# Weights of a soft mixture of experts loaded as whole experts: 2 MB transfers with 16 KB rows instead of 1 MB with 8 KB rows

## The chip, the cores and the metric

The kernel runs on one core of a Trainium2 chip. The metric is the device time of one execution in microseconds (us). On one core, a run is called slow when it is over 1.5% above the fastest run of its kernel. Six runs of the kernel before spread over 0.26 us (178.22 to 178.48), so small steps below were run several times in rounds that alternate with the kernel before, on the same chip.

## The reference, cut to what matters

Eight batches of eight heads of local attention (four heads with a window of 32, four with a dilated window), 576 tokens each, feed a soft mixture of experts with 8 experts of 4 slots.

```python
logits = x @ phi                                   # x: attention output, 4608 x 512
d = softmax of logits over the tokens
slot_input = (d.T @ x).reshape(E, S_per_e, D)      # needs all of the attention
for e in range(E):                                 # w1[e]: 512 x 1024, w2[e]: 1024 x 512, float32
    h = np.maximum(slot_input[e] @ w1[e], 0.0)
    slot_out[e] = h @ w2[e]
return softmax of logits over the slots @ slot_out # 4608 x 512 float32
```

Two things follow. The experts can't start until the attention has ended, and the output can't start until the last expert has its weights. q, k and v are 28.3 MB, w1 and w2 together 33.6 MB, the output 9.4 MB.

## The kernel before

The loads issued from POOL, all on one queue, are cast from float32 to bf16 on the way: the page of the kernel before has 30.41 MB written by that queue. Only phi and the first half expert come from SP (1.1 MB, not cast). The program is laid out at build time by a list scheduler: every operation has a priority, made of the number of its half batch (`PERIOD`) and an offset for its kind (`OFFS`); the scheduler runs a model of the engines and of the loads, and so fixes the order of instructions on each engine. Each engine then works through its list in order and waits where data is missing, as PE does 1.62 us before the first slab's work (timeline of the kernel before, below).

```python
W_AFTER = [0, 1, 1, 1, 1, 1, 1, 1, 1, 1, 1, 1, 1, 1, 1, 99]   # weight transfers after each half batch's k, q, v
PERIOD = 21.8
OFFS = dict(T=92.2, SC=104.1, EX=-30.5, MK=78.7, ...)

def w1_piece(e, hf, r0=0, n=2):                 # half an expert: partition p gets rows 2p and 2p+1, 8 KB
    def fn():
        return pool.dma_start(
            a(o_w1 + e * 4096 + hf * 2048 + 1024 * r0, [[1, 1024 * n]]),
            moe_w1[e, 256 * hf:256 * hf + 256, :].rearrange("(p two) f -> p (two f)", two=2)
            [:, 1024 * r0:1024 * (r0 + n)])
    ...
def w2_piece(e, c0):                            # half of an expert: 8 KB out of each 16 KB
    ...
def w2_slab(e, s, c0=0, n=8):                   # half of the output columns: rows of 1 KB
    ...
for e in range(8):
    wq += [w1_piece(e, x) for x in range(e == 0, 2)]
for e in range(6):
    wq += [w2_piece(e, 0), w2_piece(e, 4)]
for s in range(2):                              # experts 6 and 7: columns 0-255 first, then the rest
    wq += [w2_slab(6, s), w2_slab(7, s, 0, 4), w2_slab(7, s, 4, 2),
           w2_slab(7, s, 6, 1), w2_slab(7, s, 7, 1)]
```

The tail: `sd_fn` transposes the slot inputs (four small transposes on PE, the first work after the attention), `l1_fn` is the first expert layer (64 matmuls), `l2` the second. The last two experts' second weights come in two slabs of columns. When slab 0 is there, the left half of the output is computed for 2.5 of 9 token groups and stored ("early stores", rows of 1 KB); when slab 1 is there, the right half of the same groups and then whole rows of the others follow. The number of early groups is `NA = 2.5`.

The softmax here doesn't subtract the row's maximum and nothing guards it: scores larger than these inputs give would overflow.

## Time and profile before

| | before |
|---|---|
| time, median of 3 (178.22 to 178.29) | 178.27 us |
| span of the profile | 176.3 us |
| last load packet ends (from the packets in the trace file; no view prints it) | 152.2 us |
| first expert layer on PE | 128.1 to 131.8 us |
| DMA engines busy | all of the span, apart from its ends |

From the page of the kernel before: the span, the busy tenths of the DMA engines and what they wrote in 40 slices of 4.4 us, the packets, and the bytes at the memory.

```profile
span 176.3 us, 4802 instructions
...
DMA  5999999999999999999999999999999999999997
GB/s 182 237 211 213 216 207 213 214 209 213 215 208 214 214 208 214 214 207 215 210 209 213 211 211 216 213 216 210 217 213 211 210 192 194 298 319 415 416 427 316
DMA packets 19221, 41.26 MB, mean 234 GB/s; under 512 B 1921, under 2 KB 8577, under 8 KB 18305
...
HBM read 61.93 MB, written 9.44 MB: 405 GB/s over the span
```

The GB/s are of bytes written. A cast load writes half of what it reads (30.41 MB for 60.8 of the 61.93 MB read; the rest is SP's), so 212 GB/s in the slices of the loads are 424 GB/s read. The dip to 192 and 194 is the slabs with their 1 KB rows. Slices of 415 and more are stores, which write what they read: their transfers make 9.44 MB, as does the HBM line.

The chain of work that ended last, before: start in us, length in us, what. Its end is quoted.

```profile
119.16 33.35 DMA ar<-in_moe_w_dram
...
152.56 0.30 PE ps L858
...
152.88 0.44 DVE ar L882
...
153.81 8.63 DVE ar L914 x15
```

The last slab was issued at 119.16 us and landed 33 us later, behind everything queued ahead of it. The loads of q, k and v landed a median 21 us after their issue. So the queue is never near empty, and the end of the loads is set by bytes and by what a byte costs.

PE in the timeline of the kernel before: start, length, engine, line, operation, count, and in brackets how long PE sat idle before it and for what.

```profile
127.56 0.26 PE L802 MATMUL ps<-ar 32*128 32x32 bf16 x4 [0.77 <-DVE ar L744]
128.13 3.64 PE L819 MATMUL ps<-ar 128*32 128x512 bf16 x64 [0.32 <-DVE ar L808]
...
133.81 1.91 PE L858 MATMUL ps<-ar 128*32 128x512 bf16 x32 [0.54 <-DVE ar L843]
136.91 1.90 PE L858 MATMUL ps<-ar 128*32 128x512 bf16 x8 [1.18 <-DMA ar<-in_moe_w_dram]
...
144.43 1.05 PE L858 MATMUL ps<-ar 128*32 128x256 bf16 x8 [1.62 <-DMA ar<-in_moe_w_dram]
```

The first line is the end of the attention (127.6 us), the second the first expert layer, the third experts 0 to 3 of the second layer. From 136 us on PE waits for weights: there is slack between the attention and the weights. At 144.4 us the first slab's work begins.

### The profile page before, as it was taken

The page shows a single profiled execution, that of the slowest core. Times are in us where ns is not written, and L with a number is a line of the kernel's source. Part 1 is how long each engine was busy: PE and PEld are TensorE (multiplying, and loading weights), DVE is VectorE, ACT ScalarE, POOL GpSimd, SP SyncE. Part 2 cuts the span into 40 slices and gives each one's busy share as a digit, 9 for nine tenths or more (in the row PEclk, how much of TensorE's full clock was granted, in tenths as well). Part 3 has the DMA queues.
Part 4 walks back from the last instruction along what each step waited for, and adds up shares of the span by engine and source line. Part 5 has one row for each costly group of instructions (what it writes and reads, how often), then busy time and mean ns, then how long its engine had stood idle before and what let it go on. Part 6 is the DMA issues. An engine that isn't in the chain of part 4 may idle for free.

```text
span 176.3 us, 4802 instructions
## 1 busy us (share of the span) xinstructions
PE 126.7 (72%) x2102; PEld 85.4 (48%) x2102; DVE 119.6 (68%) x218; ACT 104.3 (59%) x165; POOL 51.1 (29%) x102
## 2 busy tenths in 40 slices
PE   0008787889798999989969989996685648897000
PEld 0005555667577767667647667674333224431000
DVE  6899396897989899999599899655400013499200
ACT  2404379888689889799669779793320012399000
POOL 7659822422422513423860000691000000000000
PEclk9999999999999999999999999999999996999855
DMA  5999999999999999999999999999999999999997
GB/s 182 237 211 213 216 207 213 214 209 213 215 208 214 214 208 214 214 207 215 210 209 213 211 211 216 213 216 210 217 213 211 210 192 194 298 319 415 416 427 316
DMA packets 19221, 41.26 MB, mean 234 GB/s; under 512 B 1921, under 2 KB 8577, under 8 KB 18305
## 3 DMA queue, kind: packets, MB, share of 16 engines
q0 software_dynamic: 15056, 30.41, 91.4%
q1 hardware_dynamic: 4144, 10.55, 15.6%
q8 instruction: 16, 0.26, 0.5%
q14 instruction: 5, 0.03, 0.0%
HBM read 61.93 MB, written 9.44 MB: 405 GB/s over the span
## 4 chain that ended last, share of the span: by engine, by line
DMA 47%; DVE 21%; PE 13%; POOL 4%; ACT 4%; issue 2%; POOLq 0%; DVEq 0%
DMA ar<-in_k_dram 28%; DMA ar<-in_moe_w_dram 19%; DVE ar L489 6%; DVE ar L914 6%; PE ps L510 4%; POOL ar L371 3%; ACT ar L549 3%; PE ps L604 2%; DVE ar L615 2%; PE ps L571 2%; DVE ar L445 2%; PE ps L517 2%; DVE ar L450 1%; PE ps L527 1%; DVE ar L495 1%
## 5 line engine op out<-in xcount | busy, mean ns | idle before, releaser
L549 ACT ACTIVATE ar<-ps 128x1152 bf16<-128x1152 f32 (+1 forms) x32 | 37.9, 1185 | 24.1 <-PE ps L534 13.4
L489 DVE STREAM_TRANSPOSE ar<-ar 128x576 uint32<-128x576 uint32 x40 | 48.6, 1241 | 3.0 <-DMA ar<-in_k_dram 2.8
L510 PE MATMUL ps<-ar 128*128 128x320 bf16 (+1 forms) x128 | 23.4, 308 | 15.7 <-DVE ar L489 13.8
L615 DVE TENSOR_TENSOR ar<-ps,fs 96x768 bf16<-96x768 f32 (+1 forms) x32 | 26.3, 822 | 1.2
L577 ACT ACTIVATE ar<-ps 128x768 bf16<-128x768 bf16 x32 | 24.9, 812 | 1.1 <-PE ps L571 1.0
L510 PEld LDWEIGHTS ps<-ar 128*128 128x128 bf16 x128 | 10.4, 100 | 20.8 <-POOL ar L418 13.7
L604 PE MATMUL ps<-ar 128*128 128x65 bf16 x320 | 15.5, 197 | 3.4 <-ACT ar L549 3.2
L571 PE MATMUL ps<-ar 128*128 128x128 bf16 x192 | 15.8, 228 | 2.8 <-DVE ar L615 1.9
L911 ACT ACTIVATE ar<-ps,fs 128x512 f32<-128x512 f32 (+1 forms) x23 | 11.5, 637 | 8.2 <-PE ps L902 8.2
L604 PEld LDWEIGHTS ps<-ar 128*128 128x128 bf16 x320 | 12.8, 100 | 6.5 <-ACT ar L549 3.8
L858 PE MATMUL ps<-ar 128*32 128x512 bf16 (+1 forms) x80 | 11.4, 352 | 5.9 <-DMA ar<-in_moe_w_dram 5.2
L335 POOL DMA_DIRECT2D ar<-in_k_dram x16 | 8.9, 554 | 23.1 <-DVE ar L489 19.7
L571 PEld LDWEIGHTS ps<-ar 128*128 128x128 bf16 x192 | 12.4, 118 | 4.3 <-DVE ar L615 2.5
L914 DVE TENSOR_SCALAR ar<-ps,fs 128x512 f32<-128x512 f32 (+1 forms) x23 | 12.7, 626 | 1.2 <-PE ps L902 1.2
L611 DVE RECIPROCAL fs<-ps 96x12 f32<-96x12 f32 (+1 forms) x32 | 6.4, 199 | 9.9 <-PE ps L604 9.3
L364 POOL DMA_DIRECT2D ar<-in_moe_w_dram x12 | 6.4, 580 | 20.8 <-DVE ar L489 20.8
L335 POOL DMA_DIRECT2D ar<-in_q_dram x16 | 8.7, 546 | 11.9 <-DVE fs L611 7.0
L902 PE MATMUL ps<-ar 128*128 128x512 bf16 (+1 forms) x46 | 10.4, 356 | 1.3 <-DVE ar L882 1.0
L335 POOL DMA_DIRECT2D ar<-in_v_dram x16 | 8.8, 549 | 8.9 <-DVE fs L611 5.5
L858 PEld LDWEIGHTS ps<-ar 128*32 128x32 bf16 x80 | 5.1, 99 | 12.0 <-DMA ar<-in_moe_w_dram 9.0
L671 ACT ACTIVATE ar<-ps 128x576 bf16<-128x576 bf16 x16 | 9.9, 656 | 1.4 <-PE ps L655 1.2
L694 PE MATMUL ps<-ar 128*128 128x288 bf16 x64 | 9.2, 287 | 1.2 <-ACT ar L678 1.2
(75 smaller groups left out, 190.6 us busy)
## 6 DMA issues: line engine op xcount, KB each, us to landing
ar<-in_moe_w_dram POOLq DMA_DIRECT2D x29, 512.0 KB, 27.0
out_dram<-ar SPq DMA_DIRECT2D x6, 1024.0 KB, 8.5
ar<-in_k_dram POOLq DMA_DIRECT2D x16, 288.0 KB, 21.1
ar<-in_q_dram POOLq DMA_DIRECT2D x16, 288.0 KB, 21.3
ar<-in_v_dram POOLq DMA_DIRECT2D x16, 288.0 KB, 21.6
out_dram<-ar SPq DMA_DIRECT2D x10, 256.0 KB, 3.5
ar<-in_moe_w_dram SPq DMA_DIRECT2D x1, 1024.0 KB, 4.8
ar<-in_moe_w_dram POOLq DMA_DIRECT2D x2, 256.0 KB, 33.0
```

Of the source, the lines that this page charges most:

```text
L335: return pool.dma_start(a(o_stg + (s * 3 + j) * 1152, [[1, 1152]]), src[b, 4 * dl:4 * dl + 4].rearrange("h (p t) d -> (h p) (t d)", p=32))
L489: return dve.transpose(au(o_dst, [[1, 18], [18, 32]]), au(src, [[32, 18], [1, 32]]))
L510: pe.matmul(pf(h, 0, [[1, W]]), a(o_id, [[1, 128]]), a(msk, [[1, W]]), start=True, stop=False)
L549: eo = op(ACT, lambda P=P, W=W: act.activation(a(P, [[W, 4], [1, W]]), AP(ps, 0, [[4096, 128], [512, 4], [1, W]]), ACTF.Exp, scale=SCALE), ...
L571: last = pe.transpose(pb(bank.idx, bb * 256 + par * 32, [[64, 4], [1, 32]]), src, a(o_id, [[1, 128]]))
L577: op(ACT, lambda t=t, bank=bank: act.activation(a(o_vb[vs] + 3 * t * VBK, [[66, 12], [2, 32], [1, 2]]), pb(bank.idx, 0, [[64, 12], [1, 32] ...
L604: last = pe.matmul(pf(bank.idx + x, 65 * t, [[1, 65]]), w, a(VB + t * VBK + 66 * h, [[1, 65]]), start=True, stop=True)
L615: op(DVE, lambda hp=hp, bank=bank: dve.tensor_tensor(a(ox + 128 * hp, [[64, 2], [256, NT], [1, 64]], 0, rows), pf(bank.idx, 0, [[512, 2], ...
L858: last = pe.matmul(pf(sobank[x].idx, 0, [[1, n]], 32 * j, 32), a(o_htz + 1024 * g + 128 * c + 32 * j, [[1, 32]]), a(w2off(e) + DM * c + co ...
L902: op(PE, lambda: pe.matmul(pf(bank.idx, 0, [[1, cw]]), a(o_et + 512 * G + j, [[4, 128]]), a(o_so + c0, [[1, cw]]), start=True, stop=True), ...
L911: op(ACT, lambda: act.activation(dst, src(), ACTF.Copy, scale=sca), actt(cw, .1), prio + .1, reads=[bank, b_rinv], writes=wr, name=f"OE{G} ...
L914: op(DVE, lambda: dve.tensor_scalar(dst, src(), sca, None, op0=AluOp.mult), dvet(cw, True) + .08, prio + .1, reads=[bank, b_rinv], writes= ...
```

## The change

Its intent: fewer and larger transfers, with longer rows. Seven pairs of w1 transfers and five pairs of w2 transfers are merged; w1's features are dealt to the partitions in fours instead of twice in twos, so that one partition's share is 16 KB in a row of memory. Seven transfers instead of fourteen go between the loads of q, k and v, and so `W_AFTER` changes; `PERIOD` and `OFFS` are set anew.

```diff
-W_AFTER = [0, 1, 1, 1, 1, 1, 1, 1, 1, 1, 1, 1, 1, 1, 1, 99]
-PERIOD = 21.8
+W_AFTER = [0, 1, 1, 0, 1, 0, 1, 0, 1, 0, 1, 0, 1, 0, 0, 99]
+PERIOD = 22.6
-OFFS = dict(T=92.2, SC=104.1, EX=-30.5, MK=78.7, ...)
+OFFS = dict(T=64.4, SC=177.5, EX=-17.6, MK=58.6, ...)
@@
+    def w1_rows(e):
+        return moe_w1[e].rearrange("(p four) f -> p (four f)", four=4)
+
+    def w1_piece(e, r0=0):
+        def fn():
+            return pool.dma_start(a(o_w1 + e * 4096 + 1024 * r0, [[1, 4096 - 1024 * r0]]),
+                                  w1_rows(e)[:, 1024 * r0:])
@@
-    for e in range(8):
-        wq += [w1_piece(e, x) for x in range(e == 0, 2)]
-    for e in range(6):
-        wq += [w2_piece(e, 0), w2_piece(e, 4)]
+    wq += [w1_piece(e, 2 if e == 0 else 0) for e in range(8)]
+    wq += [w2_piece(e) for e in range(5)] + [w2_piece(5, 0, 4), w2_piece(5, 4, 4)]
@@ the transposes of the slot inputs
-                                a(o_sdb + 256 * (c // 2) + c % 2, [[2, 128]], 0, 32),
+                                a(o_sdb + c, [[4, 128]], 0, 32),
```

More of the change, by code (lines that the diff above doesn't have):

```diff
@@ L26 @@
 LRU = 130.0
-OFFS = dict(T=92.2, SC=104.1, EX=-30.5, MK=78.7, TB=-29.0, VE=-46.3, PV=-36.7, RC=-26.4,
-            NM=-241.3, XT=-17.7, XE=8.2, LG=-77.2, EXL=95.9, ET=37.3, EE=30.2, SI=61.8, SA=58.7)
+OFFS = dict(T=64.4, SC=177.5, EX=-17.6, MK=58.6, TB=-42.6, VE=-89.4, PV=-21.2, RC=-6.8,
+            NM=-229.1, XT=-20.7, XE=15.1, LG=-37.0, EXL=132.1, ET=25.9, EE=0.6, SI=26.7, SA=50.4)
 class Buf:
@@ L351, in w_sem, with w2_piece @@
         return shared[key]
-    def w1_piece(e, hf, r0=0, n=2):
+    def w1_rows(e):
[4 more added lines that the diff above has]
+                                  w1_rows(e)[:, 1024 * r0:])
+        return (fn, (4 - r0) << 19, f"w1_{e}", [b_w1[e]])
+    def w2_piece(e, c0=0, n=8):
         def fn():
             return pool.dma_start(
-                a(o_w1 + e * 4096 + hf * 2048 + 1024 * r0, [[1, 1024 * n]]),
-                moe_w1[e, 256 * hf:256 * hf + 256, :].rearrange("(p two) f -> p (two f)", two=2)
-                [:, 1024 * r0:1024 * (r0 + n)])
-        return (fn, n << 19, f"w1_{e}{hf}", [b_w1[e]])
-    def w2_piece(e, c0):
-        def fn():
-            return pool.dma_start(
-                a(w2off(e) + c0 * DM, [[1, 4 * DM]]),
-                moe_w2[e].rearrange("(p c) f -> p (c f)", c=8)[:, c0 * DM:(c0 + 4) * DM])
-        return (fn, 1 << 20, f"w2_{e}{c0}", b_w2[e] if e < 5 else [b_w5h[c0 // 4]])
+                a(w2off(e) + c0 * DM, [[1, n * DM]]),
+                moe_w2[e].rearrange("(p c) f -> p (c f)", c=8)[:, c0 * DM:(c0 + n) * DM])
+        return (fn, n << 18, f"w2_{e}{c0}", b_w2[e] if e < 5 else [b_w5h[c0 // 4]])
     def w2_slab(e, s, c0=0, n=8):
@@ L400, in bass_dilated_sliding_attn__then__soft_moe_slots_kernel @@
         af(w2off(4), [[1, 2048]]),
-        moe_w1[0, 0:256, :].rearrange("(p two) f -> p (two f)", two=2)), .1, -200.0,
+        w1_rows(0)[:, :2048]), .1, -200.0,
        kind="dma", nbytes=1 << 20, sem=sem("s_w1f"), writes=b_w2[4], name="w1f")
```

## The prediction

> **What bounds the kernel now.** The loads. The slices of the page show the 16 DMA engines busy from first to last; its HBM line has 61.93 MB read and 9.44 MB written, 405 GB/s over the 176.3 us span. The windows view gives 204 to 221 GB/s written in every 3 us from 8 to 143 us, so about 424 GB/s read (the loads cast to half the bytes). The last load lands at about 152.5 us; 24 us of output follow. TensorE is busy up to 94%, but does not end last: the chain of waits runs from the loads of k to the issue of the last weight slabs, 33.4 us of DMA, then the output.
>
> **What the change does.** It merges seven pairs of w1 transfers and five of w2: 12 fewer DMAs, and 1536 pairs of 8 KB reads become 1536 reads of 16 KB. Bytes are the same. The slabs of experts 6 and 7 (1 KB rows), the halves of expert 5, the q, k, v loads and the stores stay. The new w1 order costs a stride in four small transposes. New offsets reorder PE, ACT and DVE before the tail. 1 MB less of weights lies ahead of the last q, k, v.
>
> **Cost.** Packet durations in the trace are linear in the bytes read: 60 ns for 1 KB, 192 for 4.5 KB, 324 for 8 KB: 22 ns plus 0.0368 ns per byte. Packets overlap: the busy shares sum to 1.06 with 8 KB rows and about 1.41 with 1 KB rows. So (estimates) an 8 KB row occupies an engine 324/1.06 = 306 ns where its bytes need 302, a 1 KB row 42.6 where they need 37.7: 4 to 5 ns per row is overhead. Merging saves 1536/16 = 96 rows per engine, 0.4 to 0.5 us. Each DMA ends with a 4 byte packet per engine of 22 ns: 12 fewer save at most 0.26 us. On POOL 12 issues of 0.54 us go, off the path: q, k, v land 21 us after issue, so the queue is never near empty. [...] here 1 MB transfers, queued back to back, already run at about 424, [...]. The 16 KB pitch is already that of w2, whose 8 KB rows take the same 324 ns as w1's, so I expect no penalty from it.
>
> **On the critical path.** All of the DMA saving, since loads run without a gap: the last load should land 0.4 to 0.7 us earlier, with the tail unchanged. The new engine order should be worth nothing: the second expert layer waits for weights from 135.7 us on (waits view, timeline), and has some 5 us of slack before the slabs.
>
> **Prediction: 177.6 us, range 176.9 to 178.5. Faster by over 2%: 0.02; within 2%: 0.95; slower by over 2%: 0.03.**
>
> **What would show it.** Right: 16 KB rows of about 625 ns; DMA share nearer 1.04 where they flow; last load 0.4 to 0.7 us earlier; 24 us from there to the end. Wrong: 16 KB packets over 650 ns or split in two; a stretch under 200 GB/s before the slabs; the first expert layer still running when the slabs land; a longer tail.
>
> **What would make it wrong.** A larger cost of 16 KB rows; lumpier q, k, v arrival that puts attention so far behind that staging frees late and the queue empties, or that the tail waits for it; a different start.

## The result, and the profile after

The changed kernel takes 177.91 us (177.79 to 178.15, 6 runs), the kernel before beside it 178.28 us (178.22 to 178.48, 6 runs). The ratio is 0.9978, with a 95% interval of 0.9965 to 0.9991: 0.39 us faster, small but clear of the noise. Ratios here are the mean time of one kernel's fast runs over that of the other's of the same rounds, so not quite the ratio of the medians.

From the page of the kernel after:

```profile
span 176.1 us, 4787 instructions
...
DMA  5999999999999999999999999999999999999997
GB/s 186 233 210 210 224 201 210 227 201 209 220 210 208 219 214 208 214 217 205 216 215 204 209 216 221 220 212 216 216 220 203 204 195 196 296 312 415 422 419 318
DMA packets 17492, 41.26 MB, mean 234 GB/s; under 512 B 1728, under 2 KB 8384, under 8 KB 15040
...
HBM read 61.93 MB, written 9.44 MB: 405 GB/s over the span
```

There are 1729 packets fewer: 1536 rows, 192 completion packets of 4 bytes (1665 of 4 bytes before, 1473 after, in the trace files: 16 for each of 12 transfers), and one other. The bytes are the same. Sizes count bytes written; packets of 8 KB or more grew from 916 (19221 less 18305) to 2452, by the 1536 merged rows. The slices move by a few GB/s up and down (201 to 227 from the third to the 25th, against 207 to 216), most likely because a slice of 4.4 us no longer holds whole transfers alike; no run isolates it.

The end of the chain, after:

```profile
120.13 32.05 DMA ar<-in_moe_w_dram
152.23 0.30 PE ps L857
152.55 0.44 DVE ar L881
...
153.48 8.64 DVE ar L913 x15
```

The chain ends through the same steps, and they start 0.33 us sooner. The loads end sooner by the same: the last load packet ends at 151.86 instead of 152.20 us. But PE before that looks different:

```profile
129.68 0.31 PE L801 MATMUL ps<-ar 32*128 32x32 bf16 x4 [0.77 <-DVE ar L743]
130.40 6.30 PE L818 MATMUL ps<-ar 128*32 128x512 bf16 x64 [0.41 <-DVE ar L807]
...
138.74 4.49 PE L857 MATMUL ps<-ar 128*32 128x512 bf16 x48 [0.54 <-DVE ar L842]
144.09 1.05 PE L857 MATMUL ps<-ar 128*32 128x256 bf16 x8 [0.85 <-DMA ar<-in_moe_w_dram]
```

The attention ends 2.1 us later than before, and the first expert layer takes 6.30 us instead of 3.64, because the granted clock was 0.78 and 0.71 of full speed in the 10 us stretches from 120 and 130 us, against 1.00 before; over the layer's own 6.30 us it was 0.57, and 0.50 in each microsecond of it up to 135 us. Experts 0 to 5 of the second layer no longer wait for weights: 48 matmuls run in one piece. Yet at 144.1 us PE waits for the first slab again. Five microseconds of lateness were swallowed by slack. The slower clock is not a property of the change: `x_slack` and `x_na35` (below), with the same loads, and `x_split2i` run the first expert layer in 3.64 us, and `x_bna35`, with the loads and nearly the order of before, takes 6.46 us.

The durations of single packets, which the trace records, grouped by the bytes read. They are medians over both traces and, for 2 KB, over an experiment below:

| row, bytes read | 1 KB | 2 KB | 4.5 KB | 8 KB | 16 KB | completion, 4 B |
|---|---|---|---|---|---|---|
| packet, ns | 60 | 98 | 192 | 324 | 625 | 22 |

All lie on one line of 22 ns and 0.0368 ns per byte; the 16 KB rows are where the prediction put them. A packet overlaps its neighbours (the packets' times sum to 1.06 of the 16 engines' time between 120 and 130 us before, and to 1.45 from 143 us, with 1 KB rows), so the 22 ns are not what a row costs; the experiments measure that.

The place where the loads give way to the stores, in windows of 1 us. Columns: window, its length, busy us of PE, its weight loads, DVE, ACT and POOL with counts, granted clock, DMA share, GB/s. Before:

```profile
153.00:154.00 1.00, 0.64 (x6) 0.64 (x7) 0.49 (x2) 0.30 (x1) 0.00 (x0) 1.00 1.07 368
154.00:155.00 1.00, 1.00 (x8) 0.66 (x7) 1.00 (x4) 1.00 (x4) 0.00 (x0) 1.00 0.59 206
155.00:156.00 1.00, 1.00 (x7) 0.42 (x6) 1.00 (x4) 1.00 (x3) 0.00 (x0) 1.00 0.95 325
```

After:

```profile
153.00:154.00 1.00, 0.96 (x9) 0.91 (x9) 0.52 (x2) 0.63 (x2) 0.00 (x0) 1.00 0.74 258
154.00:155.00 1.00, 1.00 (x7) 0.58 (x6) 1.00 (x3) 1.00 (x4) 0.00 (x0) 1.00 0.53 188
155.00:156.00 1.00, 1.00 (x6) 0.34 (x4) 1.00 (x3) 1.00 (x3) 0.00 (x0) 1.00 1.05 345
```

Between the early stores and those of the right halves there is a gap. Taking 1.05 as a full share, it is 0.5 us long before ((1.05 - 0.59) + (1.05 - 0.95), over 1.05) and 0.8 us after ((1.05 - 0.74) + (1.05 - 0.53), over 1.05). The early stores of the changed kernel begin at 149.49 instead of 150.23 us, more than the loads gained, so it is likely that they run out sooner for that; no run isolates it.

### The profile page after: what moved, and what is told of

Same layout as the page of the kernel before. It is cut to its first block, busy times and chain, and to the rows that moved or that the text cites. A ratio compares the mean times of both kernels' runs of the same rounds, so it can differ in the third digit from the quotient of the medians.

```text
span 176.1 us, 4787 instructions
## 1 busy us (share of the span) xinstructions
PE 129.5 (74%) x2102; PEld 86.8 (49%) x2102; DVE 120.5 (68%) x218; ACT 104.4 (59%) x165; POOL 44.9 (25%) x90
## 4 chain that ended last, share of the span: by engine, by line
DMA 32%; PE 23%; DVE 21%; ACT 10%; POOL 4%; issue 2%; POOLq 0%; DVEq 0%
DMA ar<-in_moe_w_dram 18%; DMA ar<-in_v_dram 14%; PE ps L509 6%; DVE ar L488 6%; DVE ar L913 6%; ACT ar L548 5%; POOL ar L372 3%; PE ps L603 3%; PE ps L570 3%; ACT ar L670 2%; PE ps L693 2%; DVE ar L614 2%; PE ps L516 2%; PE ps L526 2%; ACT ar L576 2%
## 5 line engine op out<-in xcount | busy, mean ns | idle before, releaser
L857 PE MATMUL ps<-ar 128*32 128x512 bf16 (+1 forms) x80 | 9.6, 338 | 2.9 <-DMA ar<-in_moe_w_dram 1.4
L693 PE MATMUL ps<-ar 128*128 128x288 bf16 x64 | 10.2, 307 | 1.2 <-ACT ar L677 1.2
L901 PE MATMUL ps<-ar 128*128 128x512 bf16 (+1 forms) x46 | 9.9, 340 | 1.3 <-DVE ar L881 1.0
L673 ACT ACTIVATE ar<-ps 128x1024 bf16<-128x1024 bf16 x8 | 8.2, 1030 | 2.5 <-PE ps L660 2.3
L494 DVE STREAM_TRANSPOSE ar<-ar 128x160 uint32<-128x160 uint32 (+1 forms) x32 | 9.5, 409 | 0.1
```

The costliest lines, as they stand in the source:

```text
L693: last = pe.matmul(pf(bank.idx, 0, [[1, 288]]), a(o_phis + 128 * c, [[1, 128]]), a(o_xt[xt] + 576 * c + 288 * g, [[1, 288]]), start=(c == ...
```

## The experiments

Theories to begin with:

- **Rows.** The gain comes from 96 rows fewer per DMA engine; a row costs 4 to 5 ns beyond its bytes (the prediction's estimate from packet times and shares).
- **DMA count.** It comes from 12 transfers fewer: completion packets, issue on POOL.
- **Order.** It comes from the new offsets, which reorder PE, ACT and DVE.

A question joined them when the first results came: what do the new offsets do, if they don't earn the gain?

### The order alone, and the loads alone

`x_order` is the kernel before with the new `PERIOD` and `OFFS`:

```diff
-PERIOD = 21.8
-OFFS = dict(T=92.2, SC=104.1, ...)
+PERIOD = 22.6
+OFFS = dict(T=64.4, SC=177.5, ...)
```

> The kernel before with only the new engine order (OFFS and PERIOD of the change), loads untouched. Rows theory (the gain comes from fewer, longer rows): 178.25 us, as before within 0.15 us, because the order of PE, ACT and DVE before the tail is off the critical path. DMA-count theory: also as before. Order theory (the retuned order earned the 0.37 us): about 177.9 us.

Measured: 179.74 us (179.47 to 179.78, 5 fast runs), ratio 1.0069 (1.0057 to 1.0082). No theory expected a loss of 1.2 us.

`x_loads` is the changed kernel with the old `PERIOD` and `OFFS`, the reverse of that edit.

> The changed kernel with the old OFFS and PERIOD, so the loads of the change alone. Rows theory and DMA-count theory: 177.9 us, the whole gain of 0.37 us. Order theory: about 178.25 us.

Measured: 182.61 us median, from 179.37 to 185.03 us. Only two of six runs count as fast (179.37 and 181.58); with them the ratio is 1.0114 (1.0062 to 1.0165). With so wide a spread this is the loss of the luckiest runs, and the usual loss may be larger. No theory expected that either. The profile is of a slow run, so its times are not used to compare; `x_order`, all of whose runs are fast, shows the mechanism. PE in the timeline of `x_order`:

```profile
137.58 0.26 PE L802 MATMUL ps<-ar 32*128 32x32 bf16 x4 [0.77 <-DVE ar L744]
138.15 3.64 PE L819 MATMUL ps<-ar 128*32 128x512 bf16 x64 [0.32 <-DVE ar L808]
143.84 4.97 PE L858 MATMUL ps<-ar 128*32 128x512 bf16 x64 [0.54 <-DVE ar L843]
149.86 1.05 PE L858 MATMUL ps<-ar 128*32 128x256 bf16 x8 [1.05 <-DMA ar<-in_moe_w_dram]
```

The loads of `x_order` are those of before, and the last load packet ends at 152.22 us, as before (152.20). But the attention ends at 137.6 instead of 127.6 us. When the first slab has landed, PE is still at experts 0 to 5; the first stores start at 152.7 instead of 150.2 us, the DMA engines run out of work between loads and stores (their share is 0.30 from 152 to 153 us, against 1.07 before), and the kernel ends later.

The reason lies in the build. I compared, place by place, the lists of PE operations (237 in each) that the scheduler makes. Before and after differ in 21 places. With the offsets exchanged, the list differs from that of the kernel whose loads it has in 146 places (`x_order` against before) and 143 (`x_loads` against after). So the new offsets do not bring a new order. They bring nearly the old order back, which the new load times would otherwise have changed for a worse one. The same comparison shows what the experiments below hold fixed: `x_2kb` has the lists of PE, ACT and DVE of the kernel before in every place, and all the `x_split` kernels have those of the change.

### How much lateness is free

From the trace of before: the second layer starts 6.2 us after the attention's end, experts 0 to 5 took 3.7 us once nothing kept them (143.8 to 147.5 us in `x_order`), and the first slab's work begins at 144.4 us. So an end of the attention up to about 134.4 us should cost nothing (an estimate from these numbers). `x_slack` tests it with the changed kernel and a third set of offsets:

```diff
-PERIOD = 22.6
-OFFS = dict(T=64.4, SC=177.5, EX=-17.6, MK=58.6, ...)
+PERIOD = 22.1
+OFFS = dict(T=83.3, SC=99.2, EX=-53.3, MK=50.4, ...)
```

> The changed kernel with a third set of offsets, for which the kernel's own schedule ends attention 4 us later than the change's and 5 us earlier than x_loads. Slack theory: the second expert layer's first six experts take 3.7 us once they start and are due at 144.4 us when the first slab lands, 6.2 us after attention's end; so an end of attention up to about 134.4 us costs nothing and this one, at about 133, takes 177.9 us within 0.2. If each us of lateness costs in proportion (x_loads: 9 us cost 1.5 to 5 us): 178.6 to 180 us. Where the throttle halves the clock during the first expert layer it comes 3 us later and may pass the edge by 1 to 2 us, with spread between runs.

Measured: 177.93 us (177.82 to 177.99, 5 fast runs), ratio 0.9975 (0.9962 to 0.9988). PE:

```profile
133.13 0.30 PE L800 MATMUL ps<-ar 32*128 32x32 bf16 x4 [0.77 <-DVE ar L742]
133.84 3.64 PE L817 MATMUL ps<-ar 128*32 128x512 bf16 x64 [0.41 <-DVE ar L806]
139.52 4.49 PE L856 MATMUL ps<-ar 128*32 128x512 bf16 x48 [0.54 <-DVE ar L841]
144.16 1.05 PE L856 MATMUL ps<-ar 128*32 128x256 bf16 x8 [0.15 <-DMA ar<-in_moe_w_dram]
```

The attention ends 3.5 us later than in the changed kernel, 64 of 237 places of the PE list differ, and the time is the same. The profile of the changed kernel had the slower clock, so its second layer starts only 0.8 us before this one (138.74 and 139.52 us); against the kernel before (133.81 us) it is 5.7 us. PE's wait for the first slab has shrunk to 0.15 us in this stretch: this kernel stands at the edge. The slack theory holds for the orders tried, and the order theory falls: an order earned nothing within the slack, and cost beyond it (`x_order`, second layer from 143.84 us).

### A dose of rows

`x_2k` keeps the number and size of the transfers of before, but fetches w1 of experts 1 to 7 and w2 of experts 0 to 4 as rows of 2 KB: each transfer takes every partition's 4 strided pieces instead of one run of 8 KB.

```diff
+    def w1_comb(e, x):
+        return pool.dma_start(a(o_w1 + e * 4096 + 512 * x, [[1024, 4], [1, 512]]),
+                              moe_w1[e].rearrange("(p four) f -> p four f", four=4)[:, :, 512 * x:512 * x + 512])
+    def w2_comb(e, x):
+        return pool.dma_start(a(w2off(e) + x * DM, [[2 * DM, 4], [1, DM]]),
+                              moe_w2[e].rearrange("(p c two) f -> p two c f", c=4, two=2)[:, x])
```

> Dose of row length: number of DMAs and bytes of each as before (1 MB pieces), but each partition of w1 of experts 1 to 7 and w2 of experts 0 to 4 is fetched as 4 strided rows of 2 KB instead of one of 8 KB. That is 576 rows more per DMA engine than in the kernel before. Rows theory at 4 to 5 ns a row: 2.3 to 2.9 us slower than before, about 180.8 us, packets of 2 KB with about 98 ns. DMA-count theory: as before, 178.3 us. Order theory: 177.9 us (it has the new order).

Measured: 181.99 us (181.70 to 184.02, 6 fast runs), ratio 1.0229 (1.0188 to 1.0270). The last load packet ends at 154.73 us, 2.53 us later than before, as the rows theory said. But 3.5 us or more of time were lost, not 2.5. I had given it the new offsets, which don't go with 1 MB transfers, and its attention ends at 138.7 us. `x_2kb` is the same with the old offsets.

> The 2 KB rows once more, now with the old OFFS and PERIOD, which go with 1 MB pieces. If x_2k lost 2.5 us by its rows (last load 154.7 instead of 152.2 us) and the other 1 us only because attention ended late (last transposes of the slot inputs at 138.7 instead of 127.6 us), this one ends attention before 131 us, has its last load at 154.7 us within 0.3, and takes 180.9 us (178.35 + 2.55). If 2 KB rows cost more than their load time, it stays near 182 us.

Measured: 180.49 us (180.36 to 180.66, 4 fast runs), ratio 1.0115 (1.0102 to 1.0128), so 2.0 us slower than before. The attention ends at 128.9 us, the last load packet at 154.56 us. The packets of its page:

```profile
DMA packets 28436, 41.26 MB, mean 231 GB/s; under 512 B 1920, under 2 KB 20864, under 8 KB 27520
```

There are 9215 packets more than before, 576 per engine, and the last load comes 2.36 us later (2.53 in `x_2k`): 4.1 to 4.4 ns per row. The total is 0.5 us better than I expected; of that 0.2 us are the load time itself. The rest is most likely the choice of the trace: the profiled run of the kernel before took 178.13 us, while its runs beside `x_2kb` took 178.22 to 178.78. Over the three traces with the loads of before (last load at 152.20, 152.22 and 152.55 us), and by the mean start of the slab packets (below), a row comes to 3.6 to 4.2 ns. If a row saved between 8 and 16 KB is worth as much as one between 2 and 8 KB, 96 rows give the change 0.4 us.

### A dose of transfers

`x_split8` cuts each of the changed kernel's 12 transfers of 2 MB into 8 of 16 neighbouring partitions. The rows stay at 16 KB.

```diff
+            return pool.dma_start(a(o_w1 + e * 4096, [[1, 4096]], 16 * y, 16),
+                                  w1_rows(e)[16 * y:16 * y + 16, :])
```

(The same is done for w2.)

> Dose of the number of DMAs: the changed kernel with each of its 12 transfers of 2 MB cut by partitions into 8 of 16 partitions, rows still 16 KB: 84 DMAs more, so 84 more 4 byte completion packets on each engine. Rows theory: as the change, 177.9 us, plus at most what those packets occupy. DMA-count theory with 22 ns a completion packet: 1.8 us slower, about 179.7 us; if the whole gain of 0.37 us over 12 DMAs were the count: 2.6 us slower, about 180.5 us. POOL spends some 40 us more on issues; if q, k, v come late by that, the load rate dips below 200 GB/s before 100 us.

Measured: 184.18 us median; the three fast runs are 181.31 to 183.39 us, ratio 1.0212 (1.0172 to 1.0252). The last load packet ends at 157.32 us, 5.5 us later than in the change, far more than 84 completion packets of 22 ns. Two more kernels take this apart, with transfers of every fourth partition (`x_split4i`, 36 DMAs more) and of every eighth (`x_split8i`, 84 DMAs more, as in `x_split8`).

```diff
+            return pool.dma_start(AP(ar, y * NBF + o_w1 + e * 4096, [[4 * NBF, 32], [1, 4096]]),
+                                  w1_rows(e)[y::4, :])
```

> The changed kernel with each 2 MB transfer cut into 4 DMAs of every fourth partition (32 partitions spread over all 128), rows still 16 KB: 36 DMAs more. x_split8 put its last load 5.5 us later for 84 more DMAs of 16 neighbouring partitions, 65 ns each. Theory A, a DMA costs that by itself: last load 2.3 us later than the change, about 154.2, time about 180.2 us. Theory B, neighbouring partitions were the cost of x_split8 and a DMA costs only its completion packets of at most 22 ns per engine: last load up to 0.8 us later, time 178.0 to 178.7 us, 16 KB packets at 625 ns on average as in the change instead of 644.

Measured: 178.43 us (178.35 to 178.52, 5 fast runs), ratio 1.0000 (0.9988 to 1.0012). The last load packet ends at 152.43 us, 0.57 us later than in the change: 16 ns per DMA and engine. The 16 KB packets are at 625 ns on average. Theory B holds.

> x_split8 with every eighth partition per DMA instead of 16 neighbours; same number of DMAs, same rows. If 84 DMAs at 15 ns are all there is: last load 1.3 us later than the change, about 153.1 us, 16 KB packets back at 625 to 630 ns from 644, time about 179.2 us. If DMAs of one row per engine cost more by their number, it stays at 157 us as x_split8.

Measured: 180.21 us (179.84 to 180.28, 4 fast runs), ratio 1.0099 (1.0085 to 1.0112). The last load packet ends at 154.14 us, 2.3 us later than in the change, 27 ns per DMA. That is a microsecond more than I expected. With one row per engine and DMA (16 rows and 16 completion packets in each), a DMA seems to cost more than with two, 27 ns against 16 (last loads are good to some 0.2 us, which is 6 ns per DMA in `x_split4i` and 2 ns here); why is open. The other 3.2 us of `x_split8` (157.32 against 154.14 us) come from which partitions a transfer takes, as that is all that differs. The GB/s of the slices show it; first `x_split8`:

```profile
GB/s 182 234 210 211 218 183 211 215 169 205 220 180 198 218 197 189 216 210 187 214 211 202 211 215 213 206 219 206 208 208 209 208 192 192 283 279 412 415 422 318
```

Then `x_split8i`:

```profile
GB/s 165 243 213 211 219 201 212 221 201 208 224 200 208 218 207 206 219 204 208 217 207 205 210 221 204 211 211 213 208 208 206 203 194 190 301 285 412 426 412 323
```

The dips to 169 to 189 GB/s, in slices in which w1 flows between q, k and v, are gone. The packets show the cost too: those of 16 KB took 644 ns on average with neighbours (`x_split8`) and 626 without (`x_split8i`). All of the lengthening lies before the last packet of q, k and v: there the 16 KB packets of `x_split8` average 660 ns, and that last packet ends at 111.1 us instead of 108.1 us. After it, when the queue holds nothing but weights, most of them still in transfers of 16 neighbours, they take 625 ns, and the loads up to 140 us run at 209.8 GB/s written (from the packets in the trace file), as in `x_split8i` (209.0). So neighbours cost 3 us where their transfers alternate with those of q, k and v, and nothing that the trace shows where they follow each other; why is open.

`x_split2i` cuts into two transfers of every second partition, so that rows are as in the change and the number of DMAs as before.

> The changed kernel with each of the 12 transfers of 2 MB cut into 2 DMAs of every second partition: rows of 16 KB, but as many DMAs as in the kernel before. It splits the change's two savings. From x_split4i (36 DMAs: last load 0.57 us later) a DMA costs about 15 ns per engine, from x_2kb and x_2k a row 4.1 to 4.4 ns. So last load 0.19 us later than the change, at about 152.0, and time 178.05 to 178.1 us: half to two thirds of the change's gain stays with the rows. If the gain were all rows: 177.9. If all the number of DMAs: 178.35, as before.

Measured: 178.12 us (178.09 to 178.16, 5 fast runs), ratio 0.9986 (0.9974 to 0.9998), against 0.9978 for the change. The last load packet ends at 152.13 us, 0.27 us later than in the change, 22 ns per DMA. By these totals about two thirds of the change's gain would be its rows and one third the number of DMAs, and the doses (0.4 us for 96 rows, 0.2 us for 12 DMAs) say about the same. But the intervals of the two ratios overlap, and the loads in the traces say the opposite. I took the fast traces together by their loads; the mean start of all 4096 slab packets is steadier than the end of the last one.

| loads | traces | last load packet ends, us | mean start of the slab packets, us |
|---|---|---|---|
| of before | before, `x_order`, `x_bna35` | 152.20, 152.22, 152.55 | 145.63, 145.56, 145.69 |
| 16 KB rows, DMAs as before | `x_split2i` | 152.13 | 145.47 |
| of the change | after, `x_slack`, `x_na35` | 151.86, 151.87, 151.75 | 145.16, 145.10, 145.16 |

The loads of the change come 0.5 us sooner in both columns. Of that, the 16 KB rows with the old number of DMAs bring 0.16 to 0.19 us and the smaller number of DMAs the other 0.3 us, from a single trace of `x_split2i`. That both rows and DMAs cost time is shown by the large doses; how the change's own gain splits between them stays open.

### The gap between early and late stores

`x_na35` is the changed kernel with 3.5 token groups stored early instead of 2.5.

```diff
-    NA = 2.5
+    NA = 3.5
-    for G, x in [(2, 2)] + [(G, x) for G in range(3, 9) for x in (0, 2)]:
+    for G, x in [(3, 2)] + [(G, x) for G in range(4, 9) for x in (0, 2)]:
```

> The changed kernel with the outputs of 3.5 groups instead of 2.5 stored in half-width pieces early. In the change the DMA share falls to 0.53 to 0.62 between 153.2 and 154.7 us (before: 0.60 to 0.73 between 154.0 and 155.5), because the early stores run out before the second half of the outputs is ready; the gap is about 0.8 us against 0.55 us, so 0.2 us of what the loads gained is lost there. If so, the longer early stores fill it, and the time is 177.3 to 177.7 us, [...]. If the gap costs nothing: 178.1 to 178.5 us.

Measured: 177.53 us (177.41 to 177.69, 5 fast runs), ratio 0.9951 (0.9938 to 0.9964). In the windows the gap is gone:

```profile
153.00:154.00 1.00, 1.00 (x10) 0.91 (x9) 0.68 (x2) 0.79 (x3) 0.00 (x0) 1.00 1.04 355
154.00:155.00 1.00, 0.94 (x6) 0.45 (x4) 1.00 (x4) 1.00 (x4) 0.00 (x0) 1.00 1.06 367
155.00:156.00 1.00, 0.96 (x5) 0.52 (x6) 1.00 (x3) 1.00 (x4) 0.00 (x0) 1.00 1.05 364
```

`x_bna35` makes the same edit in the kernel before.

> The kernel before with only the longer early stores of x_na35. Its gap between early and late stores is about 0.55 us against 0.8 us in the change, so the filling should bring less than the 0.5 us it brought there: about 178.0 to 178.2 us, and the distance between x_na35 and this one should be the load saving without the gap: 0.4 to 0.6 us. If the gap has no part in the change's small gain, this gains 0.5 us too (177.9) and the distance stays 0.37.

Measured: 178.04 us (177.79 to 178.23, 6 fast runs), ratio 0.9981 (0.9969 to 0.9993). The filling brings 0.3 us here and 0.5 us in the change (0.9978 to 0.9951). Without the gap the two load schemes lie 0.5 us apart (0.9951 over 0.9981 is 0.9970), with it 0.39 us. If so, the gap took some of what the loads gained. But each of these differences of differences is no larger than its interval. The traces make it smaller: from the end of the last load packet to the end of the span are 24.14 us before and 24.20 us in the change, and 23.87 us in both kernels with the longer early stores. So filling the gap is worth 0.3 us in either, and the wider gap of the change costs some 0.06 us.

### Fewer short rows at the end

`x_e6h` fetches half of expert 6's second weights as whole 8 KB rows before the slabs.

```diff
-    wq += ... [w2_piece(5, 0, 4), w2_piece(5, 4, 4)]
+    wq += ... [w2_piece(5, 0, 4), w2_piece(5, 4, 4), w2_piece(6, 0, 4)]
-        wq += [w2_slab(6, s), w2_slab(7, s, 0, 4), ...
+        wq += [w2_slab(6, s, 4, 4), w2_slab(7, s, 0, 4), ...
```

> The changed kernel with half of expert 6's second weights (features 0 to 3 of each 8) fetched as whole 8 KB rows in one transfer before the slabs, instead of 1 KB rows: 56 rows per engine fewer. Rows theory at 4.4 to 5 ns: last load 0.25 us earlier, at about 151.6 us. The first half of the output starts later, by 1 to 1.5 us, so that its stores reach further past the last load and fill the gap. Time 177.3 to 177.7 us if both hold; 177.9 us or more if the later start of the outputs leaves a gap of its own.

Measured: 177.89 us (177.55 to 178.40, 6 fast runs), ratio 0.9969 (0.9954 to 0.9983). The last load packet ends at 151.57 us, 0.29 us sooner than in the change, as the rows theory says. But the DMA share falls to 0.91 and 0.88 in the two windows from 149 us, against 1.35 and 1.25 in the change, with loads and early stores overlapping. The early stores come too late now, and the time is not clearly better than the change's. Where the runs' wide spread comes from is open.

## Why the prediction was right

The predicted 177.6 us (176.9 to 178.5) held the 177.91 us, and "within 2%" was right. The range also held the 178.28 us of the kernel before, so the total alone would not have told a gain from none; the steps have to be checked one by one.

Point by point:

- **Loads bound the kernel.** Right. The last load packet and the end of the chain moved together, by 0.34 and 0.33 us, and every large dose of rows or transfers moved both.
- **4 to 5 ns per row, 0.4 to 0.5 us.** About right, at the low edge: 3.6 to 4.4 ns in the dose of 2 KB rows, which would be 0.4 us for 96 rows. For the step from 8 to 16 KB itself it is not shown: `x_split2i`, with these rows and the DMAs of before, has its loads only 0.07 to 0.19 us sooner than before.
- **At most 0.26 us for 12 DMAs.** Right in size: 0.27 us in the pair of traces of `x_split2i` and the change (0.3 us by the means above), 0.19 us from `x_split4i`.
- **16 KB rows of about 625 ns, no penalty from the pitch.** Right: 625 ns. The DMA share between 120 and 130 us, where w2 flows, fell from 1.06 to 1.03, so packets overlap less.
- **Last load 0.4 to 0.7 us earlier.** 0.34 us at its end in this pair of profiles, 0.42 us at the first packet of the slabs (138.98 to 138.57 us), and 0.5 us as the mean of three traces against three. The first load packet of a profile moves by up to 0.3 us between kernels, so a number from one pair is good to some 0.2 us.
- **The tail unchanged.** Nearly. The gap between early and late stores grew from 0.5 to 0.8 us, but from the last load packet to the end the profiles have 24.14 and 24.20 us.
- **"The new engine order should be worth nothing."** Half right, and the weakest step. An order within the slack is worth nothing, as `x_slack` shows, and 5 us of slack was about right. But the step took for granted that the order stays good when the loads change, and that it did was luck as far as the prediction goes: the fastest run of `x_loads`, 179.37 us, lies outside its range. With the old offsets the new loads would have lost 2 us (two fast runs of `x_loads`), and the new offsets with the old loads lose 1.2 us. The offsets are there to keep the attention's end inside the slack.
- **Queue never empty.** Right: after the first slice, no slice before the slabs is under 200 GB/s.

The middle of the prediction is a gain of 0.7 us, and 0.39 us came. Most of what is missing is load saving taken too high: 0.34 to 0.5 us in the traces, where the prediction's terms add up to 0.6 to 0.7 us (0.4 to 0.5 for rows, at most 0.26 for DMAs); the tail took 0.06 us. Which of the two terms was too high stays open. The mechanism, loads that bound the kernel and get cheaper by fewer rows and fewer DMAs, is the predicted one.

A version that beats both kernels came out of this: the change with `NA = 3.5` takes 177.53 us.

## What to carry to other kernels

When transfers are queued back to back, expect merging to save only what each row and each transfer costs, here some 4 ns (measured between rows of 8 and 2 KB) and 16 to 27 ns on each engine (`x_split4i`, `x_split2i`, `x_split8i`); count them and multiply before expecting more, and take the product as an upper guess: here it gave 0.6 us, and the loads gained 0.34 to 0.5 us. In a kernel ordered at build time by a model of its loads, a change of the loads can change the order of every engine, as it did here: hold the schedule fixed or look at where the attention (or whatever feeds the tail) ends, or a loss of the order will be booked on the loads. And when loads hand over to stores, look for a gap between them; it can eat a gain, and filling it brought 0.3 to 0.5 us here where the change had brought 0.4.
